# Keeping two chunks in PSUM, a shorter gate chain and a cut last load in a squeeze-and-excite kernel

## The chip, the cores and the metric

The kernel runs on one core of one Trainium2 chip. The metric is the device time of one execution in microseconds (us). Executions of one kernel agree within about 0.3% here.

## The reference

```python
H = W = 256; C = 384; r = max(C // 16, 4)          # r = 24
# x: (1, H, W, C) bf16, w_down: (C, r), w_up: (r, C)
def reference(x, w_down, w_up):
    s = x.mean(axis=(1, 2))
    s = sigmoid(silu(s @ w_down) @ w_up)
    return x * s[:, None, None, :]
```

The input x has 50.3 MB. Every element is needed twice: once for the mean, and once for the product with s, which cannot start before the mean over all of x is known.

## The kernel before

The 65,536 pixels are cut into 64 chunks of 128 partitions times K = 8 pixels (rows, below) of 384 channels: 6144 bytes per partition, 768 KB per chunk. SBUF holds 34 chunk buffers. Pass 1 loads all chunks and sums the pixels by matmuls with a matrix of ones into one PSUM tile. After it, the last 34 chunks are still in SBUF ("resident"); the first 30 have been overwritten and are loaded again in pass 2 ("streamed").

```python
resident  = list(range(NCH - nbuf, NCH))
streamed2 = list(range(0, NCH - nbuf))
order2 = resident + streamed2            # the order of pass 2
...
# SyncE issues the loads
for i in range(NCH):
    b = bufof[i]
    if i >= nbuf:
        sp.wait_ge(sem_MM, i - nbuf + 1)
    sp.dma_start(bufs[b][:], x_chunk(i)).then_inc(sem_Lb[b], 16)
for j, i in enumerate(streamed2):        # the re-reads
    b = buf2[i]
    sp.wait_ge(sem_STb[b], 16 * store_cnt_at[order2[j]])
    sp.dma_start(bufs[b][:], x_chunk(i)).then_inc(sem_Lb[b], 16)
...
# TensorE, pass 1: 8 matmuls for each chunk
for j in range(K):
    mm = pe.matmul(ps_sum[:], ones_sb[:], bufs[b][:, j * C:(j + 1) * C], ...)
...
# VectorE, pass 2 (ScalarE issues the stores)
for n, i in enumerate(order2):
    ...
    dve.tensor_tensor(buf3d(b), buf3d(b), s_bcast, ALU.mult).then_inc(sem_MUL, 1)
```

Between the passes stands the gate chain, one small instruction after the other: ScalarE copies the mean out of PSUM, TensorE transposes it (3 matmuls), ScalarE copies the result (3 times), TensorE multiplies by w_down (3 matmuls), ScalarE takes the sigmoid, VectorE forms silu (`h_sb`) and spreads it over 128 columns (`hb_sb`), TensorE multiplies by w_up, and ScalarE takes the sigmoid into `s_sb`.

Of the kernel before, what the change touches and what calls it, by code (L numbers as in the profile page):

```python
# [10 lines left out]
def bass_standalone__se_block__vision_kernel(  # L11
# [6 lines left out]
    bf16 = mybir.dt.bfloat16  # L18
    fp32 = mybir.dt.float32
    ACT = mybir.ActivationFunctionType  # L20
    ALU = mybir.AluOpType
# [7 lines left out]
    NCH = NPIX // (P * K)  # L29
    assert C % P == 0 and C <= 512  # L30
    CT = C // P
    assert R <= P

    xf = x.rearrange("b h w c -> (b h w) c")
    of = out.rearrange("b h w c -> (b h w) c")

    def x_chunk(i):
        return xf[i * P * K:(i + 1) * P * K, :].rearrange("(p k) c -> p (k c)", p=P)

    def o_chunk(i):  # L40
        return of[i * P * K:(i + 1) * P * K, :].rearrange("(p k) c -> p (k c)", p=P)

    inv_npix = 1.0 / float(NPIX)

    with ExitStack() as ctx:
        def sb(name, shape, dt):
            return ctx.enter_context(nc.sbuf_tensor(name, shape, dt))
# [5 lines left out]
            return ctx.enter_context(nc.semaphore(name))  # L53

        ones_sb = sb("ones", [P, P], bf16)
        oneh_sb = sb("oneh", [P, 8], bf16)
        mean_sb = sb("mean_sb", [P, C], bf16)
        meanT_sb = sb("meanT_sb", [P, CT * 8], bf16)
        wdn_sb = sb("wdn_sb", [P, CT * R], bf16)
        wup_sb = sb("wup_sb", [R, C], bf16)  # L60
        sig_sb = sb("sig_sb", [R, 1], fp32)
        h_sb = sb("h_sb", [R, 1], fp32)
        hb_sb = sb("hb_sb", [R, P], bf16)
        dummy_sb = sb("dummy_sb", [P, 2], fp32)
        s_sb = sb("s_sb", [P, C], bf16)
        ps_sum = ps("ps_sum", [P, C])
        ps_mt = [ps(f"ps_mt{c}", [P, 8]) for c in range(CT)]
        ps_z = ps("ps_z", [R, 8])
        ps_u = ps("ps_u", [P, C])
        sem_W = sem("sem_W")  # L70
        sem_C = sem("sem_C")
        sem_MM = sem("sem_MM")
        sem_A2P = sem("sem_A2P")
        sem_P2A = sem("sem_P2A")
        sem_A2V = sem("sem_A2V")
        sem_V2P = sem("sem_V2P")
        sem_DV = sem("sem_DV")
        sem_MUL = sem("sem_MUL")

        chunk_bytes = K * C * 2  # L80
        nbuf = (nc.sbuf_bytes_remaining - 64) // chunk_bytes
# [6 lines left out]
        sem_STb = [sem(f"sem_ST{n}") for n in range(nbuf)]  # L88
        bufs = [sb(f"xbuf{n}", [P, K * C], bf16) for n in range(nbuf)]

        bufof = {i: i % nbuf for i in range(NCH)}
        resident = list(range(NCH - nbuf, NCH))
        streamed2 = list(range(0, NCH - nbuf))
        order2 = resident + streamed2
        buf2 = {}
        for i in resident:
            buf2[i] = bufof[i]
        for j, i in enumerate(streamed2):
            buf2[i] = buf2[order2[j]]

        lcnt = [0] * nbuf
        load_cnt_at = {}
# [2 lines left out]
            load_cnt_at[i] = lcnt[bufof[i]]  # L105
        reread_cnt_at = {}
        for i in streamed2:
            lcnt[buf2[i]] += 1
            reread_cnt_at[i] = lcnt[buf2[i]]
        scnt = [0] * nbuf  # L110
        store_cnt_at = {}
        for i in order2:
            scnt[buf2[i]] += 1
            store_cnt_at[i] = scnt[buf2[i]]
        total_stores = list(scnt)

        def buf3d(n):
            return bufs[n][:].rearrange("p (k c) -> p k c", c=C)

        s_bcast = s_sb[:].unsqueeze(1).to_broadcast([P, K, C])  # L120

        with nc.Block() as block:

            @block.sync
            def _(sp):
                for i in range(NCH):
                    b = bufof[i]
                    if i >= nbuf:
                        sp.wait_ge(sem_MM, i - nbuf + 1)
                    sp.dma_start(bufs[b][:], x_chunk(i)).then_inc(sem_Lb[b], 16)  # L130
                for j, i in enumerate(streamed2):
                    b = buf2[i]
                    sp.wait_ge(sem_STb[b], 16 * store_cnt_at[order2[j]])
                    sp.dma_start(bufs[b][:], x_chunk(i)).then_inc(sem_Lb[b], 16)

            @block.vector
            def _(dve):
                dve.memset(ones_sb[:], 1.0).then_inc(sem_C, 1)  # L138
                dve.memset(oneh_sb[:], 0.0).then_inc(sem_C, 1)
                dve.wait_ge(sem_C, 2)  # L140
                dve.memset(oneh_sb[0:1, :], 1.0).then_inc(sem_C, 1)
                dve.memset(dummy_sb[:], 0.0).then_inc(sem_C, 1)

                dve.wait_ge(sem_A2V, 1)
                dve.tensor_tensor(  # L145
                    h_sb[:], ps_z[:, 0:1], sig_sb[:], ALU.mult
                ).then_inc(sem_DV, 1)
                dve.wait_ge(sem_DV, 1)
                dve.wait_ge(sem_C, 4)
                dve.tensor_scalar(  # L150
                    hb_sb[:], ones_sb[0:R, :], h_sb[:, 0:1], None, ALU.mult
                ).then_inc(sem_V2P, 1)

                dve.wait_ge(sem_A2V, 2)
                for n, i in enumerate(order2):
                    b = buf2[i]
                    if i in reread_cnt_at:
                        dve.wait_ge(sem_Lb[b], 16 * reread_cnt_at[i])
                    dve.tensor_tensor(  # L159
                        buf3d(b), buf3d(b), s_bcast, ALU.mult  # L160
                    ).then_inc(sem_MUL, 1)

            @block.tensor
            def _(pe):
                pe.wait_ge(sem_C, 4)
                for i in range(NCH):
                    b = bufof[i]
                    pe.wait_ge(sem_Lb[b], 16 * load_cnt_at[i])
                    for j in range(K):
                        mm = pe.matmul(  # L170
                            ps_sum[:],
                            ones_sb[:],
                            bufs[b][:, j * C:(j + 1) * C],
                            start=(i == 0 and j == 0),
                            stop=(i == NCH - 1 and j == K - 1),
                        )
                    mm.then_inc(sem_MM, 1)

                pe.wait_ge(sem_A2P, 1)
                for c in range(CT):  # L180
                    mm = pe.matmul(  # L181
                        ps_mt[c][:],
                        mean_sb[:, c * P:(c + 1) * P],
                        oneh_sb[:],
                        start=True,
                        stop=True,
                    )
                mm.then_inc(sem_P2A, 1)

                pe.wait_ge(sem_A2P, 2)  # L190
                pe.wait_ge(sem_W, 32)
                for c in range(CT):
                    mm = pe.matmul(  # L193
                        ps_z[:],
                        wdn_sb[:, c * R:(c + 1) * R],
                        meanT_sb[:, c * 8:(c + 1) * 8],
                        start=(c == 0),
                        stop=(c == CT - 1),
                    )
                mm.then_inc(sem_P2A, 1)  # L200

                pe.wait_ge(sem_V2P, 1)
                pe.matmul(  # L203
                    ps_u[:], hb_sb[:], wup_sb[:], start=True, stop=True
                ).then_inc(sem_P2A, 1)

            @block.scalar
            def _(act):
                act.dma_start(
                    wdn_sb[:].rearrange("p (k r) -> p k r", r=R),  # L210
                    w_down.rearrange("(k p) r -> p k r", p=P),
                ).then_inc(sem_W, 16)
                act.dma_start(wup_sb[:], w_up).then_inc(sem_W, 16)

                act.wait_ge(sem_C, 4)
                act.activation(dummy_sb[:, 1:2], dummy_sb[:, 0:1], ACT.Sigmoid)  # L216

                act.wait_ge(sem_MM, NCH)
                act.activation(  # L219
                    mean_sb[:], ps_sum[:], ACT.Copy, scale=inv_npix  # L220
                ).then_inc(sem_A2P, 1)

                act.wait_ge(sem_P2A, 1)
                for c in range(CT):
                    ins = act.activation(  # L225
                        meanT_sb[:, c * 8:(c + 1) * 8], ps_mt[c][:], ACT.Copy
                    )
                ins.then_inc(sem_A2P, 1)

                act.wait_ge(sem_P2A, 2)  # L230
                act.activation(  # L231
                    sig_sb[:], ps_z[:, 0:1], ACT.Sigmoid
                ).then_inc(sem_A2V, 1)

                act.wait_ge(sem_P2A, 3)
                act.activation(s_sb[:], ps_u[:], ACT.Sigmoid).then_inc(sem_A2V, 1)  # L236

                for n, i in enumerate(order2):
                    b = buf2[i]
                    act.wait_ge(sem_MUL, n + 1)  # L240
                    act.dma_start(o_chunk(i), bufs[b][:]).then_inc(sem_STb[b], 16)
                for b in range(nbuf):
                    act.wait_ge(sem_STb[b], 16 * total_stores[b])

# [27 lines left out]
```

## Time and profile before

| | before |
|---|---|
| time, median (13 runs) | 313.05 us |
| end of pass 1 (last sum matmul) | 127.73 us |
| first multiply starts | 130.94 us |
| first store issued | 132.73 us |
| loads and stores of 768 KB | 94 and 64 |

Four rows from the page of the kernel before follow: the span in 40 slices of 7.8 us. A digit is the busy share in tenths; the last row is GB/s moved by all DMA queues.

```profile
PE   3976777777777777400000000000000000000000
...
DVE  0000000000000000299999999999844440000000
...
DMA  7999999999999999089999999999999999999997
GB/s 281 421 416 415 415 414 416 413 416 415 415 412 415 417 417 376 7 311 400 419 424 422 426 425 422 426 427 422 426 423 426 426 423 426 427 423 425 428 422 306
```

The DMA row is full nearly everywhere. It has one hole, in the slice with 7 GB/s. TensorE (PE) works only in pass 1 and VectorE (DVE) only in the first two thirds of pass 2.

The next two lines are from the page's list of DMA issues: transfer, issuing queue, number, size, median us from issue to landing.

```profile
xbuf<-in_x_dram SPq DMA_DIRECT2D x94, 768.0 KB, 20.9
out_dram<-xbuf ACTq DMA_DIRECT2D x64, 768.0 KB, 21.2
```

94 loads are the 64 of pass 1 and 30 re-reads. Next come stretches of the same execution (the view by windows; the first line names the columns, and the last number is GB/s).

```profile
core 0: us, PE busy (x) PEld busy (x) DVE busy (x) ACT busy (x) POOL busy (x), PEclk, DMA share, GB/s
14.00:110.00 96.00, 73.85 (x403) 35.13 (x401) 0.00 (x0) 0.00 (x0) 0.00 (x0) 1.00 1.02 415
126.20:133.00 6.80, 2.42 (x15) 1.07 (x15) 2.45 (x4) 1.46 (x6) 0.00 (x0) 0.77 0.00 0
141.00:230.00 89.00, 0.00 (x0) 0.00 (x0) 85.32 (x52) 0.00 (x0) 0.00 (x0) 0.50 1.02 422
252.00:300.00 48.00, 0.00 (x0) 0.00 (x0) 1.76 (x1) 0.00 (x0) 0.00 (x0) 0.50 1.02 424
```

Pass 1 runs at 415 GB/s, pass 2 at 422 to 424, each with the 16 DMA engines at a share of 1.02, and the hole moves nothing. The last line has almost no VectorE work: the last 48 us and more are stores only.

The hole, from the timeline (start in us, duration in us, engine, line of the kernel, operation, output<-inputs, shapes, count, and in brackets the idle time before and what ended it):

```profile
124.38 1.47 PE L170 MATMUL ps_sum<-xbuf,ones 128*128 128x384 bf16 x8 [0.42 <-DMA xbuf<-in_x_dram]
...
126.26 1.47 PE L170 MATMUL ps_sum<-xbuf,ones 128*128 128x384 bf16 x8 [0.41 <-DMA xbuf<-in_x_dram]
127.77 0.49 ACT L219 ACTIVATE mean_sb<-ps_sum 128x384 bf16<-128x384 f32 x1 [124.29 <-PE ps_sum L170]
...
128.31 0.23 PE L181 MATMUL ps_mt<-oneh,mean_sb 128*128 128x8 bf16 x3 [0.58 <-ACT mean_sb L219]
128.58 0.32 ACT L225 ACTIVATE meanT_sb<-ps_mt 128x8 bf16<-128x8 f32 x3 [0.32 <-PE ps_mt L181]
...
128.95 0.23 PE L193 MATMUL ps_z<-meanT_sb,wdn_sb 128*24 128x8 bf16 x3 [0.40 <-ACT meanT_sb L225]
129.21 0.16 ACT L231 ACTIVATE sig_sb<-ps_z 24x1 f32<-24x1 f32 x1 [0.32 <-PE ps_z L193]
129.40 0.15 DVE L145 TENSOR_TENSOR h_sb<-ps_z,sig_sb 24x1 f32<-24x1 f32 x1 [128.26 <-ACT sig_sb L231]
129.59 0.24 DVE L150 TENSOR_SCALAR hb_sb<-ones,h_sb 24x128 bf16<-24x128 bf16 x1
...
129.89 0.49 PE L203 MATMUL ps_u<-wup_sb,hb_sb 24*128 24x384 bf16 x1 [0.71 <-DVE hb_sb L150]
130.42 0.49 ACT L236 ACTIVATE s_sb<-ps_u 128x384 bf16<-128x384 f32 x1 [1.04 <-PE ps_u L203]
130.94 3.43 DVE L159 TENSOR_TENSOR xbuf<-xbuf,s_sb 128x3072 bf16<-128x3072 bf16 x2 [1.11 <-ACT s_sb L236]
132.73 0.37 ACTq L241 DMA_DIRECT2D out_dram<-xbuf  x1
```

A chunk arrives about every 1.88 us, and its 8 matmuls take 1.47 us. From the end of the sum (127.73) to s (130.91) the chain takes 3.18 us. Then the first multiply of 1.7 us stands ahead of the first store.

### The profile page before, as it was taken

How to read it: one execution, taken by the hardware profiler on the slowest of the kernel's cores; microseconds unless marked ns; L12 is line 12 of the kernel's file. 1: busy time of each engine (PE TensorE's matmuls, PEld its weight loads, DVE VectorE, ACT ScalarE, POOL GpSimd, SP SyncE). 2: the span in 40 equal slices, each digit the busy share in tenths (PEclk: the TensorE clock that was granted, in tenths of full speed). 3: DMA queues.
4: the chain of work that ended last, by engine and by line, in shares of the span. 5: the costliest groups of instructions: out<-in, count | busy, mean ns of one | idle time of the engine just before them, and what ended most of it. 6: DMA issues, size and time to landing. Idle time of an engine off the chain costs nothing.

```text
span 311.3 us, 1324 instructions
## 1 busy us (share of the span) xinstructions
PE 97.3 (31%) x519; PEld 46.2 (15%) x519; DVE 108.3 (35%) x70; ACT 2.9 (1%) x8; POOL 0.2 (0%) x4
## 2 busy tenths in 40 slices
PE   3976777777777777400000000000000000000000
PEld 1433333333333333200000000000000000000000
DVE  0000000000000000299999999999844440000000
ACT  1000000000000000100000000000000000000000
POOL 0000000000000000000000000000000000000000
PEclk9999999999999999855555555555555555555555
DMA  7999999999999999089999999999999999999997
GB/s 281 421 416 415 415 414 416 413 416 415 415 412 415 417 417 376 7 311 400 419 424 422 426 425 422 426 427 422 426 423 426 426 423 426 427 423 425 428 422 306
DMA packets 23195, 124.39 MB, mean 400 GB/s; under 512 B 2940, under 2 KB 2964, under 8 KB 23188
## 3 DMA queue, kind: packets, MB, share of 16 engines
q1 hardware_dynamic: 13536, 73.93, 58.0%
q10 hardware_dynamic: 9652, 50.37, 39.1%
q8 instruction: 4, 0.07, 0.1%
q14 instruction: 3, 0.02, 0.0%
HBM read 73.96 MB, written 50.33 MB: 399 GB/s over the span
## 4 chain that ended last, share of the span: by engine, by line
DMA 43%; DVE 24%; SPq 12%; PE 2%; issue 1%; ACT 0%
DMA xbuf<-in_x_dram 31%; DVE xbuf L159 24%; DMA out_dram<-xbuf 13%; SPq L130 12%; PE ps_sum L170 1%; PE ps_u L203 0%; ACT mean_sb L219 0%; ACT s_sb L236 0%; ACT meanT_sb L225 0%; DVE hb_sb L150 0%; PE ps_mt L181 0%; PE ps_z L193 0%; ACT sig_sb L231 0%; DVE h_sb L145 0%
## 5 line engine op out<-in xcount | busy, mean ns | idle before, releaser
L159 DVE TENSOR_TENSOR xbuf<-xbuf,s_sb 128x3072 bf16<-128x3072 bf16 x64 | 107.7, 1749 | 16.7 <-DMA xbuf<-in_x_dram 15.6
L170 PE MATMUL ps_sum<-xbuf,ones 128*128 128x384 bf16 x512 | 96.3, 333 | 31.4 <-DMA xbuf<-in_x_dram 31.4
L170 PEld LDWEIGHTS ps_sum<-xbuf,ones 128*128 128x128 bf16 x512 | 45.9, 99 | 81.5 <-DMA xbuf<-in_x_dram 49.6
L145 DVE TENSOR_TENSOR h_sb<-ps_z,sig_sb 24x1 f32<-24x1 f32 x1 | 0.1, 147 | 128.3 <-ACT sig_sb L231 128.3
L219 ACT ACTIVATE mean_sb<-ps_sum 128x384 bf16<-128x384 f32 x1 | 0.5, 491 | 124.3 <-PE ps_sum L170 124.3
L216 ACT ACT_TABLE_LOAD x1 | 1.3, 1283 | 2.0 <-issue 2.0
L203 PE MATMUL ps_u<-wup_sb,hb_sb 24*128 24x384 bf16 x1 | 0.5, 494 | 0.7 <-DVE hb_sb L150 0.7
L236 ACT ACTIVATE s_sb<-ps_u 128x384 bf16<-128x384 f32 x1 | 0.5, 490 | 1.0 <-PE ps_u L203 1.0
L138 DVE MEMSET ones<- 128x128 bf16 x1 | 0.2, 165 | 0.8 <-PEq L257 0.8
L181 PE MATMUL ps_mt<-oneh,mean_sb 128*128 128x8 bf16 x3 | 0.2, 171 | 0.6 <-ACT mean_sb L219 0.6
L193 PE MATMUL ps_z<-meanT_sb,wdn_sb 128*24 128x8 bf16 x3 | 0.2, 169 | 0.4 <-ACT meanT_sb L225 0.4
L225 ACT ACTIVATE meanT_sb<-ps_mt 128x8 bf16<-128x8 f32 x3 | 0.3, 178 | 0.3 <-PE ps_mt L181 0.3
L181 PEld LDWEIGHTS ps_mt<-oneh,mean_sb 128*128 128x128 bf16 x3 | 0.1, 97 | 1.0 <-ACT mean_sb L219 1.0
L150 DVE TENSOR_SCALAR hb_sb<-ones,h_sb 24x128 bf16<-24x128 bf16 x1 | 0.2, 242 | 0.0
L203 PEld LDWEIGHTS ps_u<-wup_sb,hb_sb 24*128 24x128 bf16 x1 | 0.1, 100 | 0.8 <-DVE hb_sb L150 0.8
L216 ACT ACTIVATE dummy_sb<-dummy_sb 128x1 f32<-128x1 f32 x1 | 0.2, 203 | 0.0
L193 PEld LDWEIGHTS ps_z<-meanT_sb,wdn_sb 128*24 128x24 bf16 x3 | 0.1, 90 | 0.5 <-ACT meanT_sb L225 0.5
L231 ACT ACTIVATE sig_sb<-ps_z 24x1 f32<-24x1 f32 x1 | 0.2, 160 | 0.3 <-PE ps_z L193 0.3
L257 POOL MEMSET const-bfloat16-1.0<- 128x1 bf16 x1 | 0.1, 101 | 0.0
L257 POOL MEMSET const-uint8-127<- 128x1 uint8 x1 | 0.1, 101 | 0.0
L257 POOL MEMSET const-float32-0.0<- 128x1 f32 x1 | 0.1, 98 | 0.2 <-issue 0.2
L257 POOL MEMSET const-float32-1.0<- 128x1 f32 x1 | 0.1, 98 | 0.0
(3 smaller groups left out, 0.2 us busy)
## 6 DMA issues: line engine op xcount, KB each, us to landing
xbuf<-in_x_dram SPq DMA_DIRECT2D x94, 768.0 KB, 20.9
out_dram<-xbuf ACTq DMA_DIRECT2D x64, 768.0 KB, 21.2
wdn_sb<-in_w_down_dram ACTq DMA_DIRECT2D x1, 18.0 KB
wup_sb<-in_w_up_dram ACTq DMA_DIRECT2D x1, 18.0 KB
```

Source lines behind the costliest of these rows:

```text
L130: sp.dma_start(bufs[b][:], x_chunk(i)).then_inc(sem_Lb[b], 16)
L138: dve.memset(ones_sb[:], 1.0).then_inc(sem_C, 1)
L159: dve.tensor_tensor(buf3d(b), buf3d(b), s_bcast, ALU.mult).then_inc(sem_MUL, 1)
L170: mm = pe.matmul(ps_sum[:], ones_sb[:], bufs[b][:, j * C:(j + 1) * C], start=(i == 0 and j == 0), stop=(i == NCH - 1 and j == K - 1),)
L181: mm = pe.matmul(ps_mt[c][:], mean_sb[:, c * P:(c + 1) * P], oneh_sb[:], start=True, stop=True,)
L193: mm = pe.matmul(ps_z[:], wdn_sb[:, c * R:(c + 1) * R], meanT_sb[:, c * 8:(c + 1) * 8], start=(c == 0), stop=(c == CT - 1),)
L203: pe.matmul(ps_u[:], hb_sb[:], wup_sb[:], start=True, stop=True).then_inc(sem_P2A, 1)
L216: act.activation(dummy_sb[:, 1:2], dummy_sb[:, 0:1], ACT.Sigmoid)
L219: act.activation(mean_sb[:], ps_sum[:], ACT.Copy, scale=inv_npix).then_inc(sem_A2P, 1)
L225: ins = act.activation(meanT_sb[:, c * 8:(c + 1) * 8], ps_mt[c][:], ACT.Copy)
L236: act.activation(s_sb[:], ps_u[:], ACT.Sigmoid).then_inc(sem_A2V, 1)
L257: nc = _bacc.Bacc("TRN2", target_bir_lowering=False, num_devices=1)
```

## The change

The intent has three parts: move fewer bytes in pass 2, shorten the chain, and let the sum of the last chunk start before all of it has landed. The diff, cut to its core and shortened:

```diff
+        ps_sum = ps("ps_sum", [P, 512])[:, 0:C]
+        ps_u = ps("ps_u", [P, 512])[:, 0:C]
+        stash = [psum_tensor(f"stash{n}", [P, K * C // 2], fp32) for n in range(2)]
+        stashed = streamed2[-2:]            # two chunks that need no re-read
+        last_split = K - 2
 # SyncE
+                    if i == last:           # 6 rows, then 2 rows on their own semaphore
+                        sp.dma_start(buf3d(b, 0, last_split), x_rows(i, 0, last_split))...
+                        sp.dma_start(buf3d(b, last_split, K), x_rows(i, last_split, K))...
 ...
                 for j, i in enumerate(streamed2):
+                    if i in stashed:
+                        continue
 # VectorE
+                for n, i in enumerate(stashed):       # in pass 1, bit for bit
+                    dve.tensor_copy(stash[n][:], bufs[bufof[i]][:].bitcast(fp32))...
+                dve.tensor_tensor_reduce(out=zscr_sb, in0=wdnT_sb[:], in1=ps_sum[0:R, :],
+                    scale=inv_npix, op0=ALU.mult, op1=ALU.add, accum_out=z_sb[:])
-                dve.tensor_tensor(h_sb[:], ps_z[:, 0:1], sig_sb[:], ALU.mult)
-                dve.tensor_scalar(hb_sb[:], ones_sb[0:R, :], h_sb[:, 0:1], None, ALU.mult)
+                dve.tensor_scalar(hb_sb[:], ones_sb[0:R, :], z_sb[:, 0:1], sig_sb[:, 0:1],
+                    ALU.mult, ALU.mult)
 ...
+                    if i in stashed:                  # pass 2 multiplies from PSUM
+                        src = stash[stashed.index(i)][:].bitcast(bf16)...
 # TensorE: w_down is transposed ahead of pass 1 (3 matmuls with an identity matrix)
-                # 3 transposes of the mean and 3 matmuls with w_down after pass 1
 # ScalarE: 3 copies of the transposed w_down at the start
-                # mean copy and 3 copies of the transposed mean after pass 1
```

The row sums stand in every partition of `ps_sum`, because the matrix of ones is 128 wide. So with w_down transposed ahead of time, one VectorE instruction over 24 partitions replaces mean copy, transposes, copies and the product with w_down.

## The prediction

> **What bounds the kernel now.** It makes two passes over x (64 chunks of 768 KB), joined by a short serial chain. The page gives 94 loads and 64 stores of 768 KB, so 34 buffers and 30 re-reads. By the slices, the DMA engines are about full (415 GB/s in pass 1, 425 in pass 2) except for one hole. PE is busy 1.47 us of each 1.88 us chunk in pass 1. DVE needs 1.75 us per chunk, finishes at 254.3 us, and then some 57 us of nothing but stores remain. So bytes bound both passes; PE and DVE matter only in the hole. [...]
>
> The hole, from the timeline: last chunk arrives 126.26, PE's last 8 matmuls end 127.75, the chain mean copy, transposes, copies, z, sigmoid, h, hb, u, sigmoid ends 130.92, first multiply ends and first store is issued 132.73. The window 126.2 to 133.0 moved 0 GB/s.
>
> **The change.**
> 1. Two streamed chunks are kept in PSUM, so 28 re-reads instead of 30. The built kernel still has 34 buffers and whole-chunk stores. Pass 2 moves 94 chunks between 133.9 and 310.0: 1.88 us each. Two fewer: -3.75 us, all on the critical path: the queues never run empty there.
> 2. Last load cut at row 6 of 8. The first part should arrive about 0.47 us (a quarter of 1.88) before the end, but PE is still on chunk 62 until 125.85. So six matmuls run 125.85 to 126.95 and two more to about 127.3: -0.4 us: PE bounds it.
> 3. Chain. Removed: mean copy 0.50, three transposes 0.24, three copies 0.32, three z matmuls 0.24, h 0.16. Added: one DVE multiply-and-sum over 24x384 from PSUM plus its accumulator read. Estimate 0.6 us: the 24x128 tensor_scalar takes 0.24, the 24x1 op 0.15[...]. PE's end to s: 3.17 us before, about 2.25 after: -0.9 us.
> 4. Moved off the path: transposing w_down at the start. The weights' last landing is near 7.1 us, so PE starts near 7.5 to 8 instead of 5.28. It gains 0.4 us per chunk and is soon level. Cost 0.
> 5. Two DVE copies into PSUM [...] in pass 1, where DVE is idle: 0. Two multiplies from PSUM: [...] They come near 250 us with 30 stores still queued: 0.
>
> Sum: -3.75 - 0.4 - 0.9 = about -5.05 us, so **308.0 us** (ratio 0.984); 8 in 10: 306.6 to 309.4. Faster by over 2%: 0.12; within 2%: 0.86; slower by over 2%: 0.02.
>
> **What would show it.** DMA issues: 92 chunk loads plus one piece, written bytes equal, read bytes down 1.57 MB. Slices still near 425 GB/s in pass 2. Timeline: last sum matmul ends about 127.3; multiply-and-sum about 0.6; first multiply starts near 129.6; span about 306.2. [...]
>
> **What would make it wrong.** The multiply-and-sum being far slower than 0.6 us; the small last piece (1536-byte descriptors) landing late; pass 2's rate differing with the mix of reads and writes; multiplies from PSUM slow enough to starve the store queue.

## The result, and the profile after

The change takes 307.13 us (median of 8 runs, 306.96 to 307.24) against 313.05 us (13 runs). The ratio is 0.9809, interval 0.9799 to 0.9818, which leaves open whether it is over 2% faster. Ratios here are the mean time of one kernel's runs over that of the other's in the same rounds, so not quite the ratio of the medians. The prediction of 308.0 us with 306.6 to 309.4 holds. But 5.92 us were saved against 5.05 expected, and the 0.87 us between them have a cause that the prediction did not have.

The DMA issues of the page after:

```profile
xbuf<-in_x_dram SPq DMA_DIRECT2D x91, 768.0 KB, 20.7
...
xbuf<-in_x_dram SPq DMA_DIRECT2D x1, 576.0 KB, 21.2
xbuf<-in_x_dram SPq DMA_DIRECT2D x1, 192.0 KB, 20.0
```

28 re-reads instead of 30, and the last load in pieces of 576 and 192 KB. The windows after, same stretches (columns as before):

```profile
14.00:110.00 96.00, 74.93 (x410) 35.79 (x407) 3.52 (x2) 0.00 (x0) 0.00 (x0) 1.00 1.02 417
126.20:133.00 6.80, 0.74 (x4) 0.11 (x2) 5.14 (x6) 0.69 (x2) 0.00 (x0) 0.76 0.25 100
141.00:230.00 89.00, 0.00 (x0) 0.00 (x0) 84.82 (x51) 0.00 (x0) 0.00 (x0) 0.50 1.02 424
```

The second line is now not empty, because stores start before 133 us. Look also at the first line: pass 1 runs at 417 GB/s instead of 415, which the change did not intend. The timeline around the hole:

```profile
123.70 2.91 PE L249 MATMUL ps_sum<-xbuf,ones 128*128 128x384 bf16 x16 [0.41 <-DMA xbuf<-in_x_dram]
...
126.65 0.55 DVE L201 CUSTOM_DVE_ANT_0 ps_u<-wdnT_sb,ps_sum 24x384 f32<-24x384 bf16 x1 [63.22 <-PE ps_sum L249]
127.13 0.13 DVE L201 DVE_READ_ACCUMULATOR2_ANT z_sb<- 24x1 f32 x1
127.29 0.20 ACT L289 ACTIVATE sig_sb<-z_sb 24x1 f32<-24x1 f32 x1 [119.08 <-DVE z_sb L201]
127.53 0.30 DVE L212 TENSOR_SCALAR hb_sb<-ones,z_sb,sig_sb 24x128 bf16<-24x128 bf16 x1 [0.27 <-ACT sig_sb L289]
...
127.88 0.33 PE L259 MATMUL ps_u<-wup_sb,hb_sb 24*128 24x384 bf16 x1 [1.27 <-DVE hb_sb L212]
128.25 0.49 ACT L292 ACTIVATE s_sb<-ps_u 128x384 bf16<-128x384 f32 x1 [0.76 <-PE ps_u L259]
128.77 3.43 DVE L226 TENSOR_TENSOR xbuf<-xbuf,s_sb 128x3072 bf16<-128x3072 bf16 x2 [0.95 <-ACT s_sb L292]
130.57 0.38 ACTq L297 DMA_DIRECT2D out_dram<-xbuf  x1
```

Chunk 62 starts at 123.70 us, not at 124.38, so pass 1 is 0.68 us ahead before the cut load plays any part. Then 16 matmuls run back to back: TensorE, which ends at 126.61 us, and not the landing of the last two rows (125.10 us by the packet records), ends pass 1. From the end of the sum (126.61) to s (128.74) the chain takes 2.13 us. The multiply-and-sum takes 0.55 us, and z is read out and used 0.64 us after its start.

Two groups of the page concern the chunks in PSUM (columns: line, engine, operation, tiles, shapes, count; total busy us and mean ns of one; idle before):

```profile
L226 DVE TENSOR_TENSOR xbuf<-xbuf,s_sb 128x3072 bf16<-128x3072 bf16 x62 | 104.1, 1749 | 11.8 <-DMA xbuf<-in_x_dram 10.8
...
L226 DVE TENSOR_TENSOR xbuf<-stash,s_sb 128x3072 bf16<-128x3072 bf16 x2 | 3.4, 1747 | 0.0
```

A multiply from PSUM takes 1747 ns, as long as one from SBUF (1749 ns).

### The profile page after: what moved, and what is told of

Read it like the earlier page. It is cut to its first block, busy times and chain, and to the rows that moved or that the text cites. A ratio compares the mean times of both kernels' runs of the same rounds, so it can differ in the third digit from the quotient of the medians.

```text
span 305.2 us, 1323 instructions
## 1 busy us (share of the span) xinstructions
PE 95.5 (31%) x516; PEld 46.0 (15%) x516; DVE 112.0 (37%) x71; ACT 2.8 (1%) x7; POOL 0.5 (0%) x5
## 4 chain that ended last, share of the span: by engine, by line
DMA 43%; DVE 23%; SPq 11%; PE 2%; DVEq 1%; issue 1%; ACT 0%
DMA xbuf<-in_x_dram 30%; DVE xbuf L226 23%; DMA out_dram<-xbuf 13%; SPq L169 11%; PE ps_sum L249 2%; DVEq L151 1%; DVE ps_u L201 0%; ACT s_sb L292 0%; PE ps_u L259 0%; DVE hb_sb L212 0%; ACT sig_sb L289 0%; DVE z_sb L201 0%
## 5 line engine op out<-in xcount | busy, mean ns | idle before, releaser
L226 DVE TENSOR_TENSOR xbuf<-xbuf,s_sb 128x3072 bf16<-128x3072 bf16 x62 | 104.1, 1749 | 11.8 <-DMA xbuf<-in_x_dram 10.8
L249 PE MATMUL ps_sum<-xbuf,ones 128*128 128x384 bf16 x512 | 94.8, 330 | 24.3 <-DMA xbuf<-in_x_dram 24.3
L197 DVE COPY stash<-xbuf 128x1536 f32<-128x1536 f32 x2 | 3.5, 1761 | 58.8 <-DMA xbuf<-in_x_dram 58.8
L226 DVE TENSOR_TENSOR xbuf<-stash,s_sb 128x3072 bf16<-128x3072 bf16 x2 | 3.4, 1747 | 0.0
```

Source lines behind the costliest of these rows:

```text
L197: dve.tensor_copy(stash[n][:], bufs[bufof[i]][:].bitcast(fp32)).then_inc(sem_SS, 1)
L226: dve.tensor_tensor(buf3d(b, r0, r1), src, s_bcast(r1 - r0), ALU.mult).then_inc(sem_MUL, 1)
```

## The experiments

All times are medians. The kernel before ran beside each call: 313.04 us in the first, 313.00 in the second, 312.99 in the third. All kernels gave correct results. The first four take the change apart; the theory is that the saving is a sum of stash, cut and chain as predicted, plus 0.6 to 0.9 us of a faster pass 1. The change itself was not run again; a run is compared with the 307.13 us of its own measurement, in which the kernel before took 313.05 us. For this faster pass 1 there were three candidates: the place of the buffers in SBUF, the later start of TensorE, and a difference between executions.

### e1: the two chunks in PSUM alone

```diff
 # the kernel before, with ps_mt, ps_z and ps_u packed into one PSUM tensor
+        stashed = streamed2[-2:]
+        # copies to PSUM, two re-reads left out, multiply from PSUM, as in the change
```

> The kernel before with the two chunks kept in PSUM and nothing else; buffers stay where they were. If each re-read is worth 1.88 us of full queues: -3.75 us against before (about 309.3 us), first store unchanged near 133.8 us, pass 2 near 172.4 us long. Rival, that the gain comes from elsewhere (the mixed part of pass 2 running at another rate): not 3.75 but clearly less (under 3.2) or more (over 4.3).

It took 309.14 us, 3.90 us less than before (ratio 0.9877). Its page shows 92 loads of whole chunks, two fewer than before:

```profile
xbuf<-in_x_dram SPq DMA_DIRECT2D x92, 768.0 KB, 20.9
```

In the packet records of the trace the first store starts at 133.54 us (133.60 before) and the stores last 172.69 us from the first to the end of the last, 3.46 us less than before. So two re-reads less are worth about what two chunks cost in full queues. The difference between e3 and e2 below gives the same step as 3.54 us; the predicted 3.75 lies between the two.

### e2: the new chain alone

```diff
-        stashed = streamed2[-2:]
+        stashed = []
-        last_split = K - 2
+        last_split = K            # and, as in e3, the branch of the cut load switched off
```

> The change without the stash and without the cut of the last load. The step of the prediction: -0.9 to -1.0 us (about 312.1), the end of the sum matmuls to s in about 2.16 us. Rival, that the 0.6 us by which pass 1 ended earlier in the profile after belongs to the change (its buffers lie 160 bytes higher in SBUF, or PE starts 2 us later): -1.6 us (about 311.4), with chunks 62 landing about 0.6 us earlier than before.

It took 311.14 us: 1.90 us less than before, where the chain alone should give 0.9 to 1.0. In its timeline pass 1 is early again:

```profile
123.71 1.47 PE L249 MATMUL ps_sum<-xbuf,ones 128*128 128x384 bf16 x8 [0.40 <-DMA xbuf<-in_x_dram]
...
125.55 1.47 PE L249 MATMUL ps_sum<-xbuf,ones 128*128 128x384 bf16 x8 [0.37 <-DMA xbuf<-in_x_dram]
```

Chunks 62 and 63 start 0.67 and 0.71 us earlier than before. This kernel has neither stash nor cut, so the faster pass 1 belongs to what it shares with the change: the later start of TensorE or the place of the buffers.

### e3: the change without the cut of the last load

```diff
-        last_split = K - 2
+        last_split = K
```

> The change without the cut of the last load. If PE bounds the end of pass 1 as predicted, the cut is worth 0.4 us: about 307.5 us. Rival, that the cut hides six of eight matmuls: 1.1 us, about 308.2.

It took 307.60 us. So the cut is worth 0.47 us (307.60 - 307.13; in the timelines the sum ends 0.43 us later, at 127.04 instead of 126.61), near the 0.4 of the argument that TensorE's backlog bounds it, and not 1.1.

### e4: the kernel before with its buffers moved by 160 bytes

```diff
         s_sb = sb("s_sb", [P, C], bf16)
+        pad_sb = sb("pad_sb", [P, 80], bf16)       # never used
```

> The kernel before with an unused tile of 160 bytes per partition ahead of the chunk buffers, which puts them at the addresses that they have after the change. If the faster pass 1 is a matter of the buffers' place: -0.6 us (about 312.4), chunk 62 landing about 0.6 us earlier. If it is a difference between executions, or comes of PE's later start: no change (within 0.2 us of before).

It took 312.18 us, 0.86 us less (ratio 0.9973, interval 0.9961 to 0.9986). An unused tile made the kernel faster. Its line of the window in pass 1, and chunk 62 in its timeline:

```profile
14.00:110.00 96.00, 74.10 (x404) 35.13 (x402) 0.00 (x0) 0.00 (x0) 0.00 (x0) 1.00 1.02 417
...
123.76 1.47 PE L171 MATMUL ps_sum<-xbuf,ones 128*128 128x384 bf16 x8 [0.41 <-DMA xbuf<-in_x_dram]
```

417 GB/s, as with the change, though TensorE starts about as early as before (5.35 us against 5.28); chunk 62 starts at 123.76 us, 0.62 us earlier than before. So the place of the buffers is the cause: the gain comes without the later start of TensorE, and the interval excludes chance (e5 below repeats it the other way round). The packet records of the trace show it directly. Each of the 128 partitions of a chunk gets its 6144 bytes as one packet (the descriptors of the recorded texts): the trace before has 20,224 packets of 6144 bytes, 128 for each of its 158 loads and stores. Between 14 and 110 us a load packet takes 239.6 ns on average before, and 238.2 ns here and with the change. Spread evenly over the 16 engines of the page, the load packets of pass 1 (64 chunks, 128 partitions) are 512 for each, which makes, as an estimate, 0.7 us of the 0.86.

The runs now split the saving into steps, each a difference of medians: place 0.86 (313.04 - 312.18), chain 1.04 (312.18 - 311.14), stash 3.54 (311.14 - 307.60), cut 0.47 (307.60 - 307.13). Their sum, 5.91 us, proves nothing: each step starts where the last one ends, so they must add up to 313.04 - 307.13. What supports them is a second measurement of each: the place 0.74 us (e5), the chain 1.05 us by the timelines, the stash 3.90 us alone (e1), the cut 0.43 us by the timelines.

### e5, e6 and e9: which places are good

What differs between byte 19680 of a partition, where the first buffer starts before the change, and byte 19840, where it starts after it? The first is a multiple of 32 and lies 224 bytes into a block of 256; the second is a multiple of 64 and lies 128 bytes into one. All buffers share this, as a chunk has 24 times 256 bytes.

```diff
 # e5, the change:            first buffer at 19936, 224 bytes into a block
+        pad_sb = sb("pad_sb", [P, 48], bf16)
 # e6, the change:            first buffer at 19968, a multiple of 256 and 512
+        pad_sb = sb("pad_sb", [P, 64], bf16)
 # e9, the kernel before:     first buffer at 19712, a multiple of 256, not of 512
+        pad_sb = sb("pad_sb", [P, 16], bf16)
```

> The change with an unused tile of 96 bytes ahead of the chunk buffers, so that they start 32 bytes off a multiple of 64, as they do before the change (and 224 bytes into a 256-byte block, as there). If that placing costs the 0.86 us seen in e4_before_shift160, this is 0.8 to 0.9 us slower than the change, about 308.0 us. If the gain of e4 was of the absolute address or of chance: 307.1 us.

> The change with 128 unused bytes ahead of the buffers, so that every descriptor starts on a multiple of 256 (and of 512) bytes in SBUF. If each step towards whole 256-byte blocks helps, faster than the change by 0.5 to 1.5 us (about 306.2). If only a multiple of 64 counts, which the change has already: 307.1 us, no change.

> The kernel before with 32 unused bytes ahead of the buffers: every descriptor then starts on a multiple of 256 bytes in SBUF, but not of 512. If a multiple of 256 is what counts, and the gain is independent of the change: pass-1 packets of 234 ns instead of 239.6, some 5.5 ns times 512 packets per engine = 2.8 to 3.2 us faster than before, about 310.0 us. If a multiple of 512 is needed: no better than the 160-byte shift, about 312.2 us.

34 buffers still fit in all three. e5 took 307.87 us, 0.74 slower than the change: taking the good place away from the change costs what giving it to the kernel before gained. Its line of the window in pass 1:

```profile
14.00:110.00 96.00, 74.81 (x410) 35.90 (x408) 3.52 (x2) 0.00 (x0) 0.00 (x0) 1.00 1.02 415
```

e6 took 304.81 us (ratio 0.9741, interval 0.9727 to 0.9754), 2.32 faster than the change:

```profile
14.00:110.00 96.00, 76.92 (x422) 37.03 (x420) 3.52 (x2) 0.00 (x0) 0.00 (x0) 1.00 1.02 424
```

e9 took 309.91 us (ratio 0.9897), 3.08 faster than before:

```profile
14.00:110.00 96.00, 75.82 (x413) 35.97 (x411) 0.00 (x0) 0.00 (x0) 0.00 (x0) 1.00 1.02 424
```

| place in the 256-byte block | kernels | load packet in pass 1 | GB/s in pass 1 |
|---|---|---|---|
| 224 | before, e5 | 239.6 ns | 415 |
| 128 | change, e4 | 238.2 ns | 417 |
| 0 | e6, e9 | 234.2 ns | 424 |

The packets are those between 14 and 110 us. A multiple of 256 was enough: e9, at an odd multiple of 256, reaches the same 234.2 ns as e6, at a multiple of 512. In e9, 6614 of the 6622 packets take 234 ns. Before, only 521 of 6479 do, and most of the others take 236 to 245 ns. So the cost lies on most packets, and not in a few long stalls. The 5.4 ns between 239.6 and 234.2 make 2.8 us over the estimated 512 packets, most of the 3.08. Places other than 0, 128 and 224 were not tried. Pass 2 shows no such difference: from the first to the last store packet it lasted 176.15 us before, 176.11 in e4 and 176.20 in e9, and re-read packets take 234 ns at the median in all of them. Why the same re-reads of the same misplaced buffers show no such cost there was not settled.

At 128 a load packet of pass 1 takes 1.7% longer than at 0, and at 224 2.3% longer. That the place is the cause is shown by the runs; by what mechanism it slows the packets was not shown.

### e7: the first multiply of pass 2 in pieces of 2, 2 and 4 rows

```diff
         p2_pieces = {i: [(0, K)] for i in order2}
+        p2_pieces[first2] = [(0, 2), (2, 4), (4, K)]
```

> The change with the first multiply of pass 2 cut in pieces of 2, 2 and 4 rows, each stored on its own. The multiply of 1.75 us stands between s and the first store; two rows should take about 0.5 us (estimate from 0.15 us fixed and 1.75 us for eight), so the first store starts 1.2 us earlier: about 305.9 us if the queues stay filled after it. If DVE, with 1.75 us per chunk against 1.88 of the queues, cannot keep them filled after the small pieces, less than 0.6 us is left.

It took 307.64 us, 0.51 slower than the change, though its first store packet came 1.11 us sooner. Three windows at the start of pass 2, first of the change:

```profile
131.00:135.00 4.00, 0.00 (x0) 0.00 (x0) 4.00 (x3) 0.00 (x0) 0.00 (x0) 0.50 0.91 369
135.00:140.00 5.00, 0.00 (x0) 0.00 (x0) 5.00 (x4) 0.00 (x0) 0.00 (x0) 0.50 1.01 366
140.00:151.00 11.00, 0.00 (x0) 0.00 (x0) 11.00 (x8) 0.00 (x0) 0.00 (x0) 0.50 1.01 408
```

Then of e7:

```profile
131.00:135.00 4.00, 0.00 (x0) 0.00 (x0) 4.00 (x3) 0.00 (x0) 0.00 (x0) 0.50 0.79 310
135.00:140.00 5.00, 0.00 (x0) 0.00 (x0) 5.00 (x4) 0.00 (x0) 0.00 (x0) 0.50 1.01 283
140.00:151.00 11.00, 0.00 (x0) 0.00 (x0) 11.00 (x8) 0.00 (x0) 0.00 (x0) 0.50 1.02 425
```

e7 moves 310 and 283 GB/s where the change moves 369 and 366. Until the first re-reads come, stores can only follow VectorE. The small pieces are stored faster than the next whole chunk is multiplied, and the packet records show no packet at all between 132.77 and 133.31 us. With the 0.24 MB that e7 had moved before 131 us, both kernels have moved 1.48 MB by 135 us: the early start is used up. The loss comes between 135 and 140 us, when the first re-reads come in. The queues are busy (share 1.01), but the packets are slow: 66 load packets take 0.3 us or more instead of 0.234, half of them over 0.55, and just one store packet starts between 135.2 and 138.1 us. The change has a dip there too, but its load packets stay at 0.23 to 0.24 us; only its stores slow down, to 0.51 us at most, and they go on. By 151 us e7 has moved 7.57 MB and the change 7.79 MB. At 425 GB/s the missing 0.22 MB are 0.5 us, which is the loss measured.

### e8: the last two loads cut finer

```diff
+        tail = {NCH - 2: [0, 4, K], NCH - 1: [0, 4, 6, K]}   # each piece with its own semaphore
```

> The change with the last two loads cut into 4+4 and 4+2+2 rows. If PE's backlog bounds the end of pass 1 (16 matmuls in a row after chunk 62 lands), PE now starts chunk 62 0.9 us earlier and ends about 0.4 to 0.5 us earlier: about 306.7 us, and the last matmuls wait for the last landing. If the small descriptors slow the queues' last part by as much: 307.1 us.

It took 306.91 us, 0.22 less than the change, half of what was expected, and hardly clear of noise: the ratios to the kernel before are 0.9805 and 0.9809, with intervals that overlap. The matmuls of the last three chunks now run as one block:

```profile
121.95 4.36 PE L247 MATMUL ps_sum<-xbuf,ones 128*128 128x384 bf16 x24 [0.41 <-DMA xbuf<-in_x_dram]
```

24 matmuls end at 126.31 instead of 126.61, 0.30 us sooner. The last packet had landed at 125.34, so they do not wait for the last landing, as had been expected: TensorE still has a backlog. Whether cutting further back would take the rest was not tried.

### e10: aligned buffers and the finer cut together

```diff
 # the change, with the pad of e6 and the tail of e8
```

> The change with 128 unused bytes ahead of the buffers (as e6) and the finer cut of the last two loads (as e8). If the two add: 304.8 minus 0.2, about 304.6 us. Since the queues now bring a chunk in 1.85 us instead of 1.88, PE's backlog at the end counts a little more, so up to 0.5 us: 304.3 to 304.6.

It took 304.32 us, ratio 0.9725 to the kernel before (interval 0.971 to 0.974). This is the fastest version; it beats the kernel before by 8.7 us and the change by 2.8. It is 0.49 faster than e6, but the runs of the two overlap (304.28 to 305.14 and 304.60 to 305.27), so the part of the finer cut is again not sure. Its timeline:

```profile
119.84 4.32 PE L248 MATMUL ps_sum<-xbuf,ones 128*128 128x384 bf16 x24 [0.42 <-DMA xbuf<-in_x_dram]
...
126.32 6.76 DVE L226 TENSOR_TENSOR xbuf<-xbuf,s_sb 128x3072 bf16<-128x3072 bf16 x4 [0.95 <-ACT s_sb L291]
```

The sum ends at 124.16 us and the first multiply starts at 126.32, 4.6 us sooner than before.

### e11: e10 with the first multiply in two halves

```diff
+        p2_pieces[first2] = [(0, 4), (4, K)]
```

> e10 with the first multiply of pass 2 in two halves of 4 rows, each stored on its own. If e7 failed because of its 1536-byte store descriptors, halves (3072 bytes) keep part of the gain: the first store 0.8 us earlier and the time 0.4 to 0.8 us below e10. If it failed because DVE's 1.67 us per chunk cannot keep the queues filled once the first pieces are stored, so that the early start is paid back, then within 0.2 us of e10 or slower.

It took 304.96 us, 0.64 slower than e10 (one of the four runs of e10, at 305.14, was as slow), while its first store packet came 0.8 us sooner. So the 1536-byte descriptors were not the whole fault of e7: with descriptors of 3072 bytes the early start is lost again, and more. The picture is that of e7: between 132.7 and 136.4 us 73 load packets take 0.3 us or more, half of them over 0.51, and no store packet starts between 132.5 and 135.9 us. In e10 stores go on in that time. Why the first re-reads are slow and hold up the stores in e7 and e11, and not in the change (0.244 us at most between 135 and 140 us), was not found. It stays open.

## Why the prediction was right, and where its sum was off

- **What bounds the kernel**: right. Bytes and their rate bound both passes (415 to 424 GB/s before, at a DMA share of 1.02), and only the hole and the first microseconds after it are open to the engines.
- **Stash (the two chunks kept in PSUM), 3.75 us**: right. 3.54 us with the other parts, 3.90 us alone.
- **Cut of the last load, 0.4 us because TensorE bounds it**: right. 0.47 us (e3); the 16 matmuls in a row show the backlog. The predicted end of the sum, 127.3 us, was 126.61, because chunks arrived 0.68 us sooner.
- **Chain, 0.9 us**: slightly low. 1.04 us by the runs and 3.18 - 2.13 = 1.05 us by the timelines. The multiply-and-sum was estimated at 0.6 us and took 0.64 until z was used.
- **"Cost 0" for the transposed w_down at the start**: right. TensorE starts its sums at 7.5 us and had caught up: in e2 it waits again for each of the last five chunks, 0.37 to 0.41 us.
- **Multiplies from PSUM slower than from SBUF**: wrong, without effect on the time; no trace or run had shown it. They took 1.75 us, as long as from SBUF, and in the trace nobody waits for them.
- **The missing term**: the prediction counted the loads of pass 1 as unchanged. It wrote "descriptors" only of the small last piece and never asked where in SBUF they land. The tiles that the change removes and adds moved every buffer by 160 bytes, and that made pass 1 faster: 0.86 us (e4). The predicted 5.05 plus 0.86 is 5.91. That fit is partly luck: the stash came out 0.21 us below its term, the chain 0.14 and the cut 0.07 above theirs, and these cancel. The range held because it was wide enough (1.4 us to each side) for the missing term.

## What to carry to other kernels

When a kernel is bound by DMA, look at the start address of its large SBUF buffers. Here 32 unused bytes that put them on a multiple of 256 gained 3.1 us, more than half of what the whole change gained, and any edit of the small tiles allocated ahead of them can move them by accident; so move them deliberately when comparing two versions. Filling free PSUM with data that would otherwise be read twice paid here, and its value was about the bytes over the rate (1.57 MB at 424 GB/s are 3.7 us; 3.5 and 3.9 were measured). Shortening the serial stretch between two full-queue phases paid too (1.04 us for 1.05 us less chain), but starting the next phase in small pieces did not (0.51 us lost in e7, 0.64 in e11): measure the bytes moved some 20 us later, not the first packet.

## What the runs measured of the hardware

- Loads of 6144-byte descriptors ran in pass 1 at 415, 417 and 424 GB/s with the SBUF buffers at 224, 128 and 0 bytes into a 256-byte block. In pass 2, with reads and writes mixed, no such cost showed (176.1 to 176.2 us for the same kernel at all three places).
- In these runs of one core 424 GB/s were read (pass 1 of e6 and e9), 424 written (252 to 300 us before) and 422 moved both ways (141 to 230 us before).
- With a bf16 source in PSUM, tensor_tensor ran as fast as from SBUF (1747 against 1749 ns for 128x3072).
- At the start of the mixed phase there can be a dip. In e7 and e11 load packets of 6144 bytes took 0.3 to 0.9 us, a few up to 1.7, instead of 0.234 for 3 to 4 us around the first re-reads, and nearly no store packet started. The kernel before has a shorter one: 29 load packets between 137.6 and 140.3 us took 0.3 us or more, up to 1.38, and for 0.89 us no store packet started.
